# Retuning the planner of a fused mLSTM, token mixer and gated MLP kernel: later first transfers, filler products in shorter gaps, one score bank moved

## The chip, the cores and the metric

The kernel runs on one core of a Trainium2 chip. The metric is the device time of one execution in microseconds (us). Shown with the kernel are three executions of the version before, and one more that the hardware profiler recorded.

## The reference

Three stages follow each other. The first is an mLSTM attention over batch 2, 8 heads, 768 steps and head size 40; the reference runs it step by step with a running maximum `m` for the exponential gates:

```python
for t in range(S):
    m_new = np.maximum(f_gate[:, :, t] + m, i_gate[:, :, t])
    f_stab = np.exp(f_gate[:, :, t] + m - m_new)
    i_stab = np.exp(i_gate[:, :, t] - m_new)
    C = f_stab * C + i_stab * outer(vt, kt);  n = f_stab * n + i_stab * kt
    y[:, :, t] = sigmoid(o_gate) * (C @ qt) / max(abs(n . qt), 1)
```

Its output, heads side by side, is x (2 x 768 x 320). Then `u = x + (relu(x.T @ w_tok1) @ w_tok2).T` and `x = u + relu(u @ w_ch1) @ w_ch2`. Last comes a gated MLP: `h = gelu(x @ w_in)` is halved into u and v, v is normalised over its 512 columns and mixed over the sequence with `w_sg` (768 x 768), and `x + (u * v_s) @ w_out` is returned in float32.

## The kernel before, in words

The attention is done in chunks of 128 steps, 6 for each batch, 12 in all (n = 0 to 11). For each chunk `p1` forms the decay matrix (L685, one product for each half of the heads, then an exponential on ScalarE and a causal mask on GpSimd, L687), `p2` forms the scores k.q (L697, eight products, four for a half) and multiplies them into the decays (L698), and `p3` weighs the values (wv, L715), updates the state (L720 and on) and forms the output (L738, L740). Ahead of that, `gates` turns the gate inputs into cumulative sums and maxima: scans on VectorE, six products L587 that spread one row over the partitions, transposes L612, L618 and L633 on TensorE, a one-column product L623, and three products L647. `spread` (L595 to L606) writes the maxima, one head after the other, into MR, which L685 reads; its wide multiplications are L605.

The weights come as float64 words. `to_f32` makes float32 of them with one pass on ScalarE and four on VectorE (L501 to L507), and `split` cuts them into a high and a low part, so that three fast products do for one exact one; the low part is a wide subtraction on line L516 (L526 and L529 in `split_tails`, L536 for the float32 weights, L977 for v, L1009 for gs). Channel mixing (`ch_steps`, L833 to L850) and the gated MLP follow the attention; weights for later stages are loaded and converted beside it.

No instruction is issued where it is written. `Plan` records every operation with its engine, a cost and its dependences, and lays them out in time by a list scheduler (`order`), with due times from a first pass; `replay` runs the found order again under a little noise, and `best` tries a grid of parameters (how early transfers may be issued, a margin for TensorE, and `big`, the widest output in elements per partition that may go to GpSimd) and keeps the order with the smallest mean. Operations written with `flex` in place of `dve` may be put on GpSimd if their output has at most `big` elements. The plan takes TensorE to run at half rate until 6.6 us (`cold`, `slow`). To keep TensorE at work ahead of its first real product it issues fillers: 128x128 products of ones (L570) into bank 7 of PSUM, until something else writes that bank:

```python
t = max([free["PE"]] + [q.end + self.LAT for q in idle.pre])
while t + idle.dur * self.cold(t) < s + 0.05:
    done.append(self.filler(t))
    t += idle.dur * self.cold(t)
```

Transfers are all issued by SyncE, in the plan's order, at most eight in flight. In `load_chunk`, qk of a chunk is three transfers of 120 KB each (L672 twice, L674), kvo one of 504 KB (L678). Scores of chunk 0 go to PSUM banks 1 and 2, those of chunk 1 to banks 6 and 7, later ones to 1 and 2 in turn; p1 has bank 0 for all.

Of the kernel before, what the change touches and what calls it, by code (L numbers as in the profile page):

```python
# [42 lines left out]
def asf(t):  # L43
    return t.bitcast(F32)
# [33 lines left out]
class Plan:  # L78
# [158 lines left out]
    def order(self, ends=None, window=9.0, margin=0.0, big=999):  # L237
# [36 lines left out]
        for _ in ops:  # L274
# [22 lines left out]
            if e == "PE" and idle is not None:  # L297
                if any(r and r[0] == idle.outs[0][0] and r[3] < idle.outs[0][4] and idle.outs[0][3] < r[4] for r in o.outs):
                    idle = None
                else:  # L300
                    t = max([free["PE"]] + [q.end + self.LAT for q in idle.pre])
                    while t + idle.dur * self.cold(t) < s + 0.05:
                        done.append(self.filler(t))
                        t += idle.dur * self.cold(t)
            o.start = s
            free[e] = s + o.dur * (self.cold(s) if e == "PE" else 1.0)
# [3 lines left out]
            if o.name == "dma_start":  # L310
                queue = max(queue, free[e] + 0.75) + o.wire * (1.0 if queue < 65.0 else 0.8)
                o.end = queue + 0.55
                lanes.append(o.end)
                lanes.sort()
# [15 lines left out]
    def replay(self, done, rand):  # L330
# [9 lines left out]
        while True:  # L340
# [35 lines left out]
            if o.name == "dma_start":  # L376
                queue = max(queue, free[e] + 0.75) + o.wire * ((1.0 if queue < 65.0 else 0.8) + 0.1 * rand())
                end[o] = queue + 0.55 + 0.3 * rand()
                lanes.append(end[o])
                lanes.sort()  # L380
# [3 lines left out]

    def best(self, rounds=2, windows=(12.0, 16.0, 20.0, 25.0, 32.0), margins=(0.0, 0.3), bigs=(400, 999), trials=6):

# [35 lines left out]
def tile_mlstm_mixer_gmlp(  # L422
# [52 lines left out]
    def bank(banks):  # L475
        i = turn.get(banks, 0)
        turn[banks] = i + 1
        return ps[:, banks[i % len(banks)], :]
# [84 lines left out]
    def gates():  # L563
# [31 lines left out]
        def spread(b, m, mr, halves):  # L595
# [7 lines left out]
            for hf in range(halves):  # L603
                hs = slice(n * hf, n * hf + n)
                dve.tensor_tensor(out=mr[:, hs, :], in0=asf(st).unsqueeze(1).to_broadcast([128, n, 128]),  # L605
                                  in1=hm[b][:, hs].unsqueeze(2).to_broadcast([128, n, 128]), op=ALU.mult)  # L606
# [83 lines left out]
    def p2(n):  # L690
        E, qt, kt = E_s[n % 4], qT[n % NSET], kTm[n % NSET]
        for hf in range(2):
            p = bank((6, 7) if n == 1 else (1, 2)).rearrange("p (j t) -> p j t", j=4)
            for j in range(4):
# [473 lines left out]
```

## Time and profile before

| what | us |
|---|---|
| three executions | 366.25, 363.68, 366.04 (median 366.04) |
| the profiled execution | 365.41 |
| its span, first to last instruction | 363.6 |
| TensorE busy in the span | 357.3 (98%) |
| VectorE busy | 261.4 (72%) |
| ScalarE busy | 167.4 (46%) |
| GpSimd busy | 86.6 (24%) |

The profiled execution is 1.8 us longer than its span; that part lies outside the program's instructions. All times in the rows below count from the start of the span. A row of the timeline merges neighbours of one form: its start, the time from the first start to the last end, engine, line, operation, output<-inputs, a form (partitions x columns) and a count. A float32 product is recorded as two passes, so that the six fillers are x12. The bracket is the idle time of the engine ahead of the row and what ended it.

### The profile page before, as it was taken

Reading aid. Unit: us, or ns where it says so; the run is one execution under the profiler, and the core shown is the slowest. Engines: PE = TensorE matmul, PEld = TensorE weight load, DVE = VectorE, ACT = ScalarE, POOL = GpSimd, SP = SyncE. Lnnn points to the kernel's source line nnn. Section 1 sums busy time; section 2 is a strip of 40 time slices with the busy share of each in tenths; the row PEclk is TensorE's granted clock in tenths of the full one; section 3 lists DMA queues with packets and bytes.
Section 4 is the critical chain, followed back from the end, with each engine's and each line's share of the span. In section 5 each row is a group of like instructions: output and inputs, shape, how many; then the busy total and the mean of one; then the engine's idle time right before and its main releaser. Section 6 shows DMA issues by size and latency. Waiting matters only on the chain.

```text
span 363.6 us, 5959 instructions
## 1 busy us (share of the span) xinstructions
PE 357.3 (98%) x2257; PEld 343.6 (95%) x2257; DVE 261.4 (72%) x510; ACT 167.4 (46%) x377; POOL 86.6 (24%) x103
## 2 busy tenths in 40 slices
PE   7999999999999999999999999999999999999996
PEld 6998988998999999999999999999999999999995
DVE  4498888899888447794673359889898887454563
ACT  4488636767353235342352338754644444122230
POOL 3172325226120000120030006972124402010100
PEclk9999999999999999999999999999999999999999
DMA  5966447792580003000480000000000010010101
GB/s 159 289 257 214 145 133 275 227 321 62 176 342 0 2 0 115 2 0 3 146 303 0 3 0 2 0 0 2 1 2 0 2 54 1 2 54 3 54 0 56
DMA packets 11238, 30.96 MB, mean 85 GB/s; under 512 B 1481, under 2 KB 4233, under 8 KB 11209
## 3 DMA queue, kind: packets, MB, share of 16 engines
q1 hardware_dynamic: 11208, 30.57, 25.5%
q8 instruction: 18, 0.29, 0.3%
q14 instruction: 12, 0.09, 0.1%
HBM read 28.60 MB, written 1.97 MB: 84 GB/s over the span
## 4 chain that ended last, share of the span: by engine, by line
PE 95%; DVE 2%; DMA 1%; ACT 1%; SPq 0%; issue 0%
PE ps L697 6%; PE ps L850 6%; PE ps L848 6%; PE ps L849 6%; PE ps L740 5%; PE ps L835 5%; PE ps L834 5%; PE ps L833 5%; PE ps L1004 5%; PE ps L1003 5%; PE ps L1002 5%; PE ps L781 4%; PE ps L838 2%; PE ps L837 2%; PE ps L685 2%; PE ps L1020 2%
## 5 line engine op out<-in xcount | busy, mean ns | idle before, releaser
L784 ACT ACTIVATE a<-ps 128x384 fp32r<-128x384 f32 x48 | 23.6, 492 | 57.5 <-PE ps L838 57.0
L785 DVE SCALAR_TENSOR_TENSOR a<-ps,a 128x384 fp32r<-128x384 f32 x48 | 26.6, 554 | 27.1 <-ACT a L784 26.4
L788 DVE TENSOR_TENSOR nat<-ps,nat 128x320 f32<-128x320 f32 x48 | 22.3, 489 | 14.5 <-PE ps L850 7.3
L1002 PE MATMUL ps<-wsg,v 128*128 128x384 f32 x96 | 32.3, 337 | 0.0
L1003 PE MATMUL ps<-wsg,v 128*128 128x384 f32 x96 | 32.3, 337 | 0.0
L1004 PE MATMUL ps<-wsg,v 128*128 128x384 f32 x96 | 32.3, 337 | 0.0
L697 PEld LDWEIGHTS ps<-qk 120*128 120x128 f32 (+1 forms) x192 | 27.9, 209 | 2.5 <-DMA qk<-in_qk_dram 1.2
L697 PE MATMUL ps<-qk 120*128 120x128 f32 (+1 forms) x192 | 29.4, 296 | 0.7 <-DMA qk<-in_qk_dram 0.7
L687 POOL TENSOR_SCALAR_AFFINE_SELECT E<-E 128x512 f32<-128x512 f32 x24 | 17.0, 717 | 43.3 <-ACT E L686 37.0
L1008 ACT CAST gs<-g 128x384 fp32r<-128x384 f32 x16 | 8.2, 512 | 36.2 <-DVE g L1007 36.2
L740 PE MATMUL ps<-kvo,E 128*128 128x41 f32 x192 | 23.2, 279 | 0.0
L740 PEld LDWEIGHTS ps<-kvo,E 128*128 128x128 f32 x192 | 22.8, 192 | 0.1
L951 ACT ACTIVATE sq<-sq 128x384 f32<-128x384 f32 (+1 forms) x28 | 15.9, 570 | 10.3 <-DVE sq L950 10.0
L949 ACT ACTIVATE sq<-ps 128x384 f32<-128x384 f32 (+1 forms) x28 | 15.0, 536 | 12.2 <-PE ps L967 9.2
L1006 DVE SCALAR_TENSOR_TENSOR g<-ps,gln,bsg 128x384 f32<-128x384 f32 x16 | 9.8, 615 | 14.6 <-PE ps L1004 14.6
L950 DVE SCALAR_TENSOR_TENSOR sq<-sq,ps 128x384 f32<-128x384 f32 (+1 forms) x28 | 17.0, 606 | 3.5 <-ACT sq L949 3.2
L698 DVE TENSOR_TENSOR E<-ps,E 128x512 f32<-128x512 f32 x24 | 16.2, 682 | 3.0 <-PE ps L697 2.4
L1002 PEld LDWEIGHTS ps<-wsg,v 128*128 128x128 f32 x96 | 18.1, 188 | 0.0
L1004 PEld LDWEIGHTS ps<-wsg,v 128*128 128x128 f32 x96 | 18.0, 188 | 0.0
L1003 PEld LDWEIGHTS ps<-wsg,v 128*128 128x128 f32 x96 | 18.0, 188 | 0.0
L801 DVE TENSOR_TENSOR uT<-ps,uT 128x384 fp32r<-128x384 f32 x24 | 13.3, 553 | 6.5 <-ACT uT L800 6.5
L686 ACT ACTIVATE E<-ps 128x512 f32<-128x512 f32 x24 | 14.3, 596 | 6.0 <-PE ps L685 5.8
(346 smaller groups left out, 1128.0 us busy)
## 6 DMA issues: line engine op xcount, KB each, us to landing
kvo<-in_kvo_dram SPq DMA_DIRECT2D x12, 504.0 KB
qk<-in_qk_dram SPq DMA_DIRECT2D x36, 120.0 KB
rwin<-in_win_dram SPq DMA_DIRECT2D x5, 512.0 KB
rwsg<-in_wsg_dram SPq DMA_DIRECT2D x6, 384.0 KB
out_dram<-nat SPq DMA_DIRECT2D x12, 160.0 KB
rwo<-in_wout_dram SPq DMA_DIRECT2D x4, 320.0 KB
rw__129<-in_tok_dram SPq DMA_DIRECT2D x1, 768.0 KB
rw__131<-in_tok_dram SPq DMA_DIRECT2D x1, 768.0 KB
```

The lines of the kernel that those rows point to most:

```text
L697: mm(p[:, j, :], kt[jj][0:r, g, :], qt[0:r, g, :], start=True, stop=True)
L740: mm(psO[:, h, :], E[:, h // 4, h % 4, :], v1[:, h, :], start=(c == 0 and h == 0), stop=(h == H - 1))
L784: act.activation(out=hi, in_=p, func=AF.Relu)
L785: dve.scalar_tensor_tensor(out=lo, in0=p, scalar=0.0, in1=asf(hi), op0=ALU.max, op1=ALU.subtract)
L788: dve.tensor_tensor(out=nat[:, b, s], in0=p, in1=nat[:, b, s], op=ALU.add)
L833: mm(p, w[:, 0, ms], hi[:, k, ts], start=(k == 0), stop=False)
L848: mm(acc, a[:, 0, js], w[:, 0, :], start=(m == 0), stop=False)
L849: mm(acc, a[:, 0, js], w[:, 1, :], start=False, stop=False)
L850: mm(acc, a[:, 1, js], w[:, 0, :], start=False, stop=(m == 5))
L1002: mm(p, v[:, 0, ds_], wsg[s][:, 0, ts], start=(s == 0), stop=False)
L1003: mm(p, v[:, 0, ds_], wsg[s][:, 1, ts], start=False, stop=False)
L1004: mm(p, v[:, 1, ds_], wsg[s][:, 0, ts], start=False, stop=(s == NC - 1))
```

## The change

Four edits, all to what the planner is told. First transfers: one that starts while the queue stands between 3.5 and 12 us costs 1.3 times its wire time, and one that ends its wire time between 3.5 and 20 us lands 1.6 us later instead of 0.55, in `order` and in `replay`. Fillers: ahead of 7.0 us a filler is put in whenever 0.2 us are left, and it may push the next product back (`s = max(s, t)`); after that the rule is nearly the old one. The grid of `best` drops the window 12.0 and gains the margin 0.15. In `spread`, the wide multiplication is `flex`; in `p2`, only the first half of chunk 1 goes to bank 6 and the second half to banks 1 and 2 in turn, so that bank 7 is written by fillers until token mixing.

```diff
-                    while t + idle.dur * self.cold(t) < s + 0.05:
+                    while t + (0.2 if t < 7.0 else idle.dur * self.cold(t) - 0.05) < s:
                         done.append(self.filler(t))
                         t += idle.dur * self.cold(t)
+                    s = max(s, t)
...
-                queue = max(queue, free[e] + 0.75) + o.wire * (1.0 if queue < 65.0 else 0.8)
-                o.end = queue + 0.55
+                queue = max(queue, free[e] + 0.75)
+                queue += o.wire * (0.8 if queue > 65.0 else 1.3 if 3.5 < queue < 12.0 else 1.0)
+                o.end = queue + (1.6 if 3.5 < queue < 20.0 else 0.55)
...
-    def best(self, rounds=2, windows=(12.0, 16.0, 20.0, 25.0, 32.0), margins=(0.0, 0.3), bigs=(400, 999), trials=6):
+    def best(self, rounds=2, windows=(16.0, 20.0, 25.0, 32.0), margins=(0.0, 0.15, 0.3), bigs=(400, 999), trials=6):
...
-                dve.tensor_tensor(out=mr[:, hs, :], in0=asf(st).unsqueeze(1).to_broadcast([128, n, 128]),
+                flex.tensor_tensor(out=mr[:, hs, :], in0=asf(st).unsqueeze(1).to_broadcast([128, n, 128]),
...
-            p = bank((6, 7) if n == 1 else (1, 2)).rearrange("p (j t) -> p j t", j=4)
+            p = bank((6,) if n == 1 and not hf else (1, 2)).rearrange("p (j t) -> p j t", j=4)
```

The edits to `replay` are the same as the second piece, with its noise. The program has the same instructions as before but for one filler; their order and the engine of some change everywhere. Lines of the changed kernel from L386 on are three higher than those before (L570 is L573).

TensorE at the start of the program, before: gt, con and qk are the gate tiles, the constants and the q and k of a chunk (qk_75 chunk 0, qk_76 chunk 1); MR_72 and LR_69 go into the decays.

```order
L570 MATMUL ps_58<-gt_111 128x128 x6
L612 MATMUL ps_58<-con_59,gt_118 1x128
L587 MATMUL ps_58<-gt_115,con_59 128x128
L697 MATMUL ps_58<-qk_75 128x128
L618 MATMUL ps_58<-con_59,gt_120 1x128
L587 MATMUL ps_58<-gt_116,con_59 128x128
L697 MATMUL ps_58<-qk_75 128x128
L623 MATMUL ps_58<-gt_111,gt_121 128x1
L697 MATMUL ps_58<-qk_75 128x128 x2
L587 MATMUL ps_58<-gt_116,con_59 128x128
L685 MATMUL ps_58<-MR_72,LR_69 128x512
```

TensorE at the same place in the changed kernel:

```order
L573 MATMUL ps_58<-gt_111 128x128 x6
L615 MATMUL ps_58<-con_59,gt_118 1x128
L573 MATMUL ps_58<-gt_111 128x128
L590 MATMUL ps_58<-gt_115,con_59 128x128
L590 MATMUL ps_58<-gt_116,con_59 128x128
L621 MATMUL ps_58<-con_59,gt_120 1x128
L700 MATMUL ps_58<-qk_75 128x128 x2
L590 MATMUL ps_58<-gt_116,con_59 128x128
L688 MATMUL ps_58<-MR_72,LR_69 128x512
L626 MATMUL ps_58<-gt_111,gt_121 128x1
L700 MATMUL ps_58<-qk_75 128x128 x2
```

One filler now stands behind the first transpose, the second L587 (L590) moved ahead of the second transpose, and both ahead of the first score product; the first L685 (L688) comes before the one-column product.

SyncE's queue of transfers from the start, before:

```order
L541 DMA gin<-in_gates_dram 128x293
L542 DMA con<-in_gates_dram 128x268
L672 DMA qk<-in_qk_dram 40x768 x2
L674 DMA qk<-in_qk_dram 40x2x384
L678 DMA kvo<-in_kvo_dram 128x1008
L672 DMA qk<-in_qk_dram 40x768 x2
L674 DMA qk<-in_qk_dram 40x2x384
L496 DMA rw__129<-in_tok_dram 128x1536
L672 DMA qk<-in_qk_dram 40x768 x2
L674 DMA qk<-in_qk_dram 40x2x384
L678 DMA kvo<-in_kvo_dram 128x1008 x2
L496 DMA rw__131<-in_tok_dram 128x1536
```

And in the changed kernel:

```order
L544 DMA gin<-in_gates_dram 128x293
L545 DMA con<-in_gates_dram 128x268
L675 DMA qk<-in_qk_dram 40x768 x2
L677 DMA qk<-in_qk_dram 40x2x384
L675 DMA qk<-in_qk_dram 40x768 x2
L677 DMA qk<-in_qk_dram 40x2x384
L681 DMA kvo<-in_kvo_dram 128x1008
L675 DMA qk<-in_qk_dram 40x768 x2
L677 DMA qk<-in_qk_dram 40x2x384
L681 DMA kvo<-in_kvo_dram 128x1008
L499 DMA rw__129<-in_tok_dram 128x1536
L681 DMA kvo<-in_kvo_dram 128x1008
```

The values of chunk 0 (kvo) moved behind the qk of chunk 1, and the first token weights (rw) behind the kvo of chunk 1; the first five transfers stand as before.

GpSimd in the gated MLP's weights, before: wsg, win and v are the spatial weights, the input weights and the normalised half of h, each with its low part subtracted here.

```order
L974 TENSOR_TENSOR mv<-mv,mhalf 128x1
L516 TENSOR_TENSOR win<-wt,win 128x512
L536 TENSOR_TENSOR wsg<-rwsg,wsg 128x768
L516 TENSOR_TENSOR win<-wt,win 128x512
L977 TENSOR_TENSOR v<-v_178,v 128x512
L536 TENSOR_TENSOR wsg<-rwsg,wsg 128x768
```

In the changed kernel, VectorE at the weights of channel mixing; L788 is L785 of before (the low part of an activation) and L519 is L516:

```order
L788 SCALAR_TENSOR_TENSOR a<-ps,a 128x384
L507 SCALAR_TENSOR_TENSOR wt<-rc__207,wt 128x384
L519 TENSOR_TENSOR c__212<-wt,c__212 128x640
L507 SCALAR_TENSOR_TENSOR wt<-rc__209,wt 128x384
L788 SCALAR_TENSOR_TENSOR a<-ps,a 128x384
```

Of all outputs wider than 400 elements, none is left on GpSimd but the masks L687 and the memsets at the start: 23 wide subtractions (seven of L516, one of L526, two of L529, five of L536, eight of L977) moved to VectorE, among them that of c__212 and those of wsg, win and v shown. Six narrower operations moved the other way (two each of L715, L732 and L1009). The wide multiplications of `spread` (512 and 1024 elements) are on VectorE in both.

## Rows read from the trace of the kernel before

**Rows 1.** The page's first part: busy us (share of the span) xinstructions of each engine.
```profile
PE 357.3 (98%) x2257; PEld 343.6 (95%) x2257; DVE 261.4 (72%) x510; ACT 167.4 (46%) x377; POOL 86.6 (24%) x103
```

**Rows 2.** Who waited for whom, TensorE alone: us in total, times, longest.
```profile
PE ps L697 <- DMA qk<-in_qk_dram: 0.7, 2, 0.4
PE ps L685 <- ACT E L686: 0.6, 1, 0.6
PE ps L794 <- DVE nat L788: 0.3, 1, 0.3
```

**Rows 3.** The timeline of TensorE over the first 19 us.
```profile
1.10 2.93 PE L570 MATMUL ps<-gt 128*128 128x128 f32 x12 [1.10 <-DVE gt L569]
3.85 0.40 PE L612 MATMUL ps<-con,gt 128*1 128x128 f32 x1
4.37 0.79 PE L587 MATMUL ps<-gt,con 128*128 128x128 f32 x2
5.46 0.76 PE L697 MATMUL ps<-qk 80*128 80x128 f32 x2 [0.29 <-DMA qk<-in_qk_dram]
...
7.25 0.79 PE L697 MATMUL ps<-qk 120*128 120x128 f32 x2 [0.39 <-DMA qk<-in_qk_dram]
...
14.77 1.49 PE L697 MATMUL ps<-qk 120*128 120x128 f32 x6
16.05 0.63 PE L587 MATMUL ps<-gt,con 128*128 128x128 f32 x2
...
16.76 0.76 PE L685 MATMUL ps<-MR,LR 128*128 128x512 f32 x1
17.33 1.08 PE L697 MATMUL ps<-qk 120*128 120x128 f32 x8
18.24 0.38 PE L720 MATMUL ps<-wv,kvo 128*120 128x123 f32 x2
18.38 0.47 PE L685 MATMUL ps<-MR,LR 128*128 128x512 f32 x1
18.69 0.55 PE L720 MATMUL ps<-wv,kvo 128*120 128x123 f32 x4
```

**Rows 4.** Windows: length, busy (x) of PE, PEld, DVE, ACT, POOL, PEclk, DMA share, GB/s.
```profile
0.00:17.30 17.30, 15.39 (x62) 13.83 (x63) 8.59 (x27) 7.65 (x19) 4.28 (x11) 1.00 0.80 217
17.30:60.00 42.70, 42.67 (x334) 39.77 (x333) 36.89 (x67) 29.23 (x76) 19.72 (x27) 1.00 0.60 204
100.00:300.00 200.00, 200.00 (x1214) 194.50 (x1213) 147.95 (x280) 89.43 (x186) 45.20 (x48) 1.00 0.13 44
```

**Rows 5.** The timeline of the other engines over the first 19 us.
```profile
0.88 0.17 DVE L569 MEMSET gt<- 128x128 f32 x1 [0.88 <-PEq L1152]
1.12 0.38 DVE L558 MEMSET qk<- 120x384 f32 x1
10.15 0.47 ACT L705 ACTIVATE th<-kvo 128x320 f32<-128x320 f32 x1 [2.69 <-DMA kvo<-in_kvo_dram]
18.82 0.75 POOL L715 TENSOR_TENSOR wv<-kvo,wT 128x328 f32<-128x328 f32 x1
```

**Rows 6.** Groups by line and form: xcount | busy us, mean ns | idle before us <-releasers.
```profile
L977 POOL TENSOR_TENSOR v<-v,v 128x512 fp32r<-128x512 f32 x8 | 10.6, 1325 | 10.3 <-ACT v L976 10.3
L977 DVE TENSOR_TENSOR v<-v,v 128x512 fp32r<-128x512 f32 x4 | 2.7, 686 | 0.0
L536 DVE TENSOR_TENSOR wsg<-rwsg,wsg 128x768 fp32r<-128x768 f32 x1 | 0.9, 946 | 0.0
L516 DVE TENSOR_TENSOR c__206<-wt,c__206 128x384 fp32r<-128x384 f32 x1 | 0.6, 553 | 0.0
```

**Rows 7.** The timeline of three engines around one wide subtraction on GpSimd.
```profile
83.44 0.55 DVE L507 SCALAR_TENSOR_TENSOR wt<-rc__136,wt 128x384 int32<-128x384 int32 x1
83.44 2.22 POOL L529 TENSOR_TENSOR c__142<-wt,c__142 64x768 fp32r<-64x768 f32 x1 [0.28 <-ACT c__142 L527]
83.91 2.17 DVE L507 SCALAR_TENSOR_TENSOR wt<-rc__138,wt 128x384 int32<-128x384 int32 x1
87.30 0.41 PE L794 MATMUL ps<-con,nat 128*128 128x128 f32 x2 [0.32 <-DVE nat L788]
```

More of the change, by code (lines that the diff above doesn't have):

```diff
@@ L376, in replay @@
             if o.name == "dma_start":
-                queue = max(queue, free[e] + 0.75) + o.wire * ((1.0 if queue < 65.0 else 0.8) + 0.1 * rand())
-                end[o] = queue + 0.55 + 0.3 * rand()
+                queue = max(queue, free[e] + 0.75)
+                queue += o.wire * ((0.8 if queue > 65.0 else 1.3 if 3.5 < queue < 12.0 else 1.0) + 0.1 * rand())
+                end[o] = queue + (1.6 if 3.5 < queue < 20.0 else 0.55) + 0.3 * rand()
                 lanes.append(end[o])
```

## The prediction, made before the changed kernel was run

> **What bounds the kernel now.** I read the page's busy shares first [rows 1]: TensorE (PE) is busy for 357.3 of 363.6 us. The waits of PE come next [rows 2], and they are small: 0.7 us for q and k, 0.6 and 0.3 us later on. So hardly any time is idle, and what can be won must lie inside the busy time. The timeline of the first 19 us [rows 3] shows it. Passes of one form, 128 columns, run from 14.77 to 16.05 in six steps, 0.213 us each; eight of them from 17.33 to 18.24, 0.114 us each. From 17.33 us on PE works at twice its former rate: before that it had the lower of its two clock levels (1.2 GHz), after it the higher (2.4 GHz). The granted clock in the windows says 1.00 for both stretches [rows 4]; the spacing contradicts it for the first, and I go by the spacing. So PE spends the time from 1.10 to 17.33, 16.2 us, at the lower level, and each microsecond by which the clock rises sooner is worth half a microsecond, as long as PE has work at hand.
>
> What PE did before the rise: fillers from 1.10 and the first transpose, then an idle 0.12 us (3.85 + 0.40 to 4.37), 0.29 us ahead of 5.46 and 0.39 us ahead of 7.25; after that no row up to 17.33 has an idle mark [rows 3]. The three short pauses are what the change's filler rule and its later transfers aim at.
>
> **The change, part by part.** The sum is made against the profiled execution, 365.4 us (span 363.6 and 1.8 outside it). That lies 0.6 us under the median of the runs shown, 366.04; I add this at the end.
>
> *Start, fillers, first transposes.* In the changed order VectorE clears qk (0.38 us) before it makes the ones for the fillers [rows 5], so the fillers begin at about 1.48, not 1.10. Six of them and the way to the transpose took 2.75 us (1.10 to 3.85): the transpose comes at 4.23. The seventh filler is two passes, 0.43 us, and with the transpose's pass 0.21: L587 at 4.87 instead of 4.37. The second L587 and the second transpose follow (0.64), then the first score product, which needs only the first two parts of qk (there before 5.46), at 5.95 to 6.4. All this is without a pause, so PE runs unbroken from 1.48 to 6.4: 4.9 us, against 3.15 (1.10 to 4.25) before. Then the next score product needs the third part of qk, which ended a wait at 7.25 before; the five transfers up to it stand as they did, so I let it land then too, and PE has one pause of 0.8 us. At 7.25 both kernels have the same real products behind them (two L587, both transposes, one score product). The filler and the later start therefore cost nothing: they lie in time that ends with that transfer. Without this cover they would cost 0.5 us.
>
> *From 7.25 to the first L720.* By the two orders PE does the same products here, except that before, a third L685 (0.57 us, 16.76 to 17.33 [rows 3]) came ahead of L720, and now behind. Before: 18.24 - 7.25 = 11.0 us, so 10.4 now at the same clock. That is no gain by itself: the L685 is done a little later.
>
> *The clock.* The trace can't show when it will rise. One bound is no gain: the rise at 17.3 as now, or even later (each microsecond costs 0.5). The other is a rise in the first unbroken run, before 7.25: then all the work up to L720 runs at the higher level, and (17.3 - 7.25)/2 = 5.0 us are won. Longer unbroken work before 6.4, and a moment that no longer follows three pauses, speak for sooner; the second pause of 0.8 us, longer than any before, speaks against the first bound. I take the middle of 6.4 and 17.3, 11.9: (17.3 - 11.9)/2 = **-2.7 us**.
>
> The Trainium skill (TensorE: Matmul & The Clock Gate, Part 1) says that the throttled clock is the default, that activity releases it and that the moment differs from run to run; and it advises against this kind of work: the ramp's penalty is under 1% of a typical span, which one is not to fit to. By that the whole penalty here would be under 3.6 us and my step about -1.2 us. The trace has 16.2 us at the lower level [rows 3], half of that 8.1 us or 2.2%, so it disagrees, and I keep -2.7. With the run-to-run part the runs do fit: 366.25 to 363.68 is 2.6 us, what a rise 5 us sooner would give.
>
> *Do the transfers and VectorE let PE have that?* kvo of chunk 0 landed at 10.15 [rows 5]. It now stands behind the three qk transfers of chunk 1, 360 KB more; at the 217 GB/s of these 17 us [rows 4] that is 1.7 us: 11.8. With wv on GpSimd (0.75 us [rows 5]) L720 can start at 12.6; with the clock up at 11.9 PE gets there at 7.25 + 4.65 + (10.4 - 4.65)/2 = 14.8, so this is hidden by 2.2 us. Bounds of the landing: 10.15, and 13.5 if it took as long again. VectorE is busy 45.5 us of the first 60 [rows 4]; in 57.3 us that is 79%, still below PE. The first token weights now stand behind kvo of chunk 1 and two transfers more, 864 KB or some 4 us at the same rate; their first user L781 stands among the L740 of chunk 2 in the changed order, two chunks behind, so I count nothing; uncovered it would be at most those 4 us. The remaining swaps of SyncE's queue lie under stages in which PE waits for no transfer [rows 2]: no cost, and none can be gained.
>
> *Subtractions to VectorE.* 23 wide ones move. On VectorE they cost 0.69 (L977, eight: 5.5 us), 0.95 (L536, five: 4.7) and between 0.55 and 0.95, say 0.8, for the ten others (8.0) [rows 6]; six operations of about 0.55 go the other way (-3.3). VectorE gets 14.9 us more, 276 of 363. Most lie between 100 and 300 us, where it is busy 148 of 200 [rows 4]. Upper bound: all of it on the path, +14.9. Lower bound: one row says a little gain. While GpSimd made L529 (83.44 to 85.66), an L507 on VectorE took 2.17 us, where its twin just ahead took 0.55 [rows 7]; the 0.3 us that PE waited for VectorE at 87.30 came behind it and may go: -0.3. VectorE already carries 14 such subtractions with no other wait of PE for it in the waits [rows 2], so I stay near the low end: one of the moved ones, say 0.8 us, lands ahead of an L785 that a product waits for (in the changed order that of c__212 stands two rows ahead of one): **+0.8 us**.
>
> *No cost, no gain:* `spread` may go to GpSimd but doesn't (its outputs are wider than the limit chosen). Bank 7 kept free lets more fillers in, and none was put in there; the second half of chunk 1's scores now shares banks 1 and 2 with chunk 0, and waits for the multiplication L698 of that. That L698 belongs to the scores at the head of the queue, so it is done while PE makes the scores between; only where PE is fast from the start can a wait show, and I leave that to the first rival.
>
> Sum: 365.4 - 2.7 + 0.8 = 363.5; with the 0.6 by which the median lies above the profiled execution, **364.1 us**, 0.5% under 366.04. About 1% is what a measurement of this kernel tells from no change.
>
> **Rivals.**
> *Early rise.* The clock rises in the unbroken first run, by 6.4. For it: 4.9 us without a pause where there were 3.15. Then PE wins 5.0, but meets L720 at 7.25 + 5.2 = 12.45 just as kvo allows it (12.6), and the transfers that reuse the qk of chunk 0 have less room; I leave 4.4 of the 5.0: 365.4 - 4.4 + 0.8 + 0.6 = 362.4.
> *No sooner rise.* The pause of 0.8 us ahead of 7.25 undoes the fillers' work, and the rise comes at 17.3 or later. For it: before, PE also went ten microseconds without an idle mark from 7.25 and stayed at the lower level all that time [rows 3]. Then only the moved subtractions count: 365.4 + 0.8 + 0.6 = 366.8; a rise 1 us later still, 367.3.
> *VectorE becomes the bound: slower.* The place is the weight conversion beside channel mixing and the gated MLP, 100 to 300 us, where the products wait for L785 behind a subtraction. It decides once more than 2.7 us of the 14.9 come onto the path. With half of it: 365.4 - 2.7 + 7.5 + 0.6 = 370.8. Against it: 52 us of VectorE's 200 are free there [rows 4], and GpSimd no longer holds it up.
>
> **How the numbers follow.** Forecast 0.48, early rise 0.18, no sooner rise 0.24, VectorE the bound 0.10. The forecast's own range is 363 to 365.5 (rise between 9 and 14 us). The whole range goes from 362.0 (early rise with the waits' lower bound) to 367.3 (late rise), and leaves out half of VectorE's case and a third of the early rise and some of the tails. Faster by over 1% is under 362.4: half of the early rise and the edge of the forecast, 0.14. Slower by over 1%, above 369.7: most of VectorE's case, 0.07. Within 1%: 0.79.
>
> **What would show it.** Right: passes of 128 columns at 0.11 us by some 12 us in TensorE's timeline, one pause ahead of the third part of qk and none before it; first L720 near 15; VectorE busy some 272 to 277 us and PE's waits for it about 1 us. The clock step is wrong if the spacing is still 0.213 at 16 us (then no gain), or 0.11 at 7.5. The transfer step is wrong if L720 waits for wv or kvo; the step on VectorE if L848 to L850 or L833 wait for L785 by more than 2 us in sum.

## The result: 360.48 us, and the profile after

Median 360.48 us (four executions, 360.14 to 361.08) against 365.64 for the kernel before beside it (363.68 to 366.25): ratio 0.987, 95% interval [0.983, 0.991]. That is under the forecast's range (362.0 to 367.3). The profiled execution took 360.39, its span is 358.7: 4.93 less than before. Medians and ratios here and below leave out slow executions, those over 1.5% above the fastest of the same kernel. Lines from L386 on are three higher now.

The page's busy shares [rows 1], then who TensorE waited for [rows 2]: us in total, times, longest.

```profile
PE 350.9 (98%) x2259; PEld 338.9 (94%) x2259; DVE 266.6 (74%) x527; ACT 168.1 (47%) x377; POOL 57.0 (16%) x86
```
```profile
PE ps L700 <- DMA qk<-in_qk_dram: 0.9, 1, 0.9
PE ps L700 <- DVE E L701: 0.6, 1, 0.6
PE ps L836 <- DVE a L788: 0.5, 1, 0.5
PE ps L797 <- DVE nat L791: 0.3, 1, 0.3
PE ps L818 <- DVE hl L788: 0.3, 1, 0.3
```

TensorE has 6.4 us less busy time for the same products and one filler more. Its waits are longer than before, and still the kernel is faster. The start of TensorE's timeline [rows 3]:

```profile
1.51 2.93 PE L573 MATMUL ps<-gt 128*128 128x128 f32 x12 [1.51 <-DVE gt L623]
4.23 0.42 PE L615 MATMUL ps<-con,gt 128*1 128x128 f32 x1
4.44 0.64 PE L573 MATMUL ps<-gt 128*128 128x128 f32 x2
4.87 0.72 PE L590 MATMUL ps<-gt,con 128*128 128x128 f32 x4
5.43 0.27 PE L621 MATMUL ps<-con,gt 128*1 128x128 f32 x1
5.54 0.39 PE L700 MATMUL ps<-qk 80*128 80x128 f32 x2
6.82 0.49 PE L700 MATMUL ps<-qk 120*128 120x128 f32 x2 [0.89 <-DMA qk<-in_qk_dram]
...
10.79 2.25 PE L700 MATMUL ps<-qk 80*128 80x128 f32 x18
12.88 0.59 PE L723 MATMUL ps<-wv,kvo 128*120 128x123 f32 x4
...
14.16 1.02 PE L743 MATMUL ps<-kvo,E 128*128 128x41 f32 x8
```

Four passes of L590 take 4.87 to 5.43, and L621's single pass only 0.11 (5.43 to 5.54): the spacing changes from 0.21 to 0.11 inside the row of L590, at 5.1 us. From there TensorE works at the higher level (eighteen passes from 10.79 in 2.09 us), which before it reached at 17.33. The first pause comes later, 0.89 us ahead of 6.82, and the clock stays up through it. The first window [rows 4] and GpSimd's step ahead of L723 (kvo was there at 10.63, forecast 11.8 [rows 5]):

```profile
0.00:17.30 17.30, 14.72 (x105) 13.71 (x105) 13.10 (x34) 10.76 (x29) 6.08 (x14) 1.00 0.75 243
```
```profile
10.63 0.74 POOL L718 TENSOR_TENSOR wv<-kvo,wT 128x328 f32<-128x328 f32 x1 [1.47 <-DMA kvo<-in_kvo_dram]
```

TensorE makes 105 passes in the first 17.3 us, not 62. Where the time went, by the starts of the same passes in both timelines:

| pass | before | after | difference |
|---|---|---|---|
| first L720 | 18.24 | 12.88 | -5.36 |
| 65th of the scores L697 | 35.6 | 31.2 | -4.44 |
| 129th | 61.2 | 56.6 | -4.63 |
| 161st | 78.1 | 72.4 | -5.77 |
| first L963 | 211.2 | 206.4 | -4.90 |
| end | 363.6 | 358.7 | -4.93 |

The prize falls in the first 13 us. Some is lost to the wait of 0.56 us at 23.58 (L700 for L701); some comes in where before's wait of 0.60 for E [rows 2] is not there; 0.27 and 0.52 are lost again to L788 at 98.1 and 102.8.

The rise at 17.33 is that of one execution of before. Of the 95 others that stand beside the runs below, 43 show a granted clock, averaged over the span, of 0.984 to 0.995, where the profiled one shows 0.998. Since the column reads 1.00 ahead of the first rise, the clock of these 43 had risen and fallen again. They took no less time (median 365.23 against 365.06 for the rest).

### The profile page after: what moved, and what is told of

It reads as the page before. It is cut to its first block, busy times and chain, and to the rows that moved or that the text cites. A ratio compares the mean times of both kernels' runs of the same rounds, so it can differ in the third digit from the quotient of the medians.

```text
span 358.7 us, 5943 instructions
## 1 busy us (share of the span) xinstructions
PE 350.9 (98%) x2259; PEld 338.9 (94%) x2259; DVE 266.6 (74%) x527; ACT 168.1 (47%) x377; POOL 57.0 (16%) x86
## 4 chain that ended last, share of the span: by engine, by line
PE 90%; DVE 4%; DMA 3%; issue 1%; ACT 1%; SPq 0%
PE ps L853 6%; PE ps L852 6%; PE ps L851 6%; PE ps L700 5%; PE ps L743 5%; PE ps L1007 5%; PE ps L836 5%; PE ps L1006 5%; PE ps L1005 5%; PE ps L837 5%; PE ps L838 5%; PE ps L784 3%; PE ps L840 2%; PE ps L841 2%; PE ps L1023 2%; PE ps L1021 2%
## 5 line engine op out<-in xcount | busy, mean ns | idle before, releaser
L787 ACT ACTIVATE a<-ps 128x384 fp32r<-128x384 f32 x48 | 23.6, 491 | 51.8 <-PE ps L841 51.4
L788 DVE SCALAR_TENSOR_TENSOR a<-ps,a 128x384 fp32r<-128x384 f32 x48 | 26.4, 554 | 22.0 <-ACT a L787 21.7
L791 DVE TENSOR_TENSOR nat<-ps,nat 128x320 f32<-128x320 f32 x48 | 22.3, 490 | 15.2 <-PE ps L853 7.3
L700 PE MATMUL ps<-qk 120*128 120x128 f32 (+1 forms) x192 | 27.0, 277 | 1.5 <-DMA qk<-in_qk_dram 0.9
L700 PEld LDWEIGHTS ps<-qk 120*128 120x128 f32 (+1 forms) x192 | 25.2, 191 | 2.8 <-DMA qk<-in_qk_dram 1.1
L952 ACT ACTIVATE sq<-ps 128x384 f32<-128x384 f32 (+1 forms) x28 | 14.9, 534 | 19.5 <-PE ps L970 14.2
L976 POOL TENSOR_SCALAR mv<-mv 128x1 f32<-128x1 f32 x12 | 4.5, 373 | 98.2 <-DVE mv L975 98.2
L1009 DVE SCALAR_TENSOR_TENSOR g<-ps,gln,bsg 128x384 f32<-128x384 f32 x16 | 9.9, 616 | 13.1 <-PE ps L1007 13.0
L701 DVE TENSOR_TENSOR E<-ps,E 128x512 f32<-128x512 f32 x24 | 16.2, 685 | 3.5 <-PE ps L700 2.4
```

Of the source, the lines that this page charges most:

```text
L700: mm(p[:, j, :], kt[jj][0:r, g, :], qt[0:r, g, :], start=True, stop=True)
L787: act.activation(out=hi, in_=p, func=AF.Relu)
L788: dve.scalar_tensor_tensor(out=lo, in0=p, scalar=0.0, in1=asf(hi), op0=ALU.max, op1=ALU.subtract)
L791: dve.tensor_tensor(out=nat[:, b, s], in0=p, in1=nat[:, b, s], op=ALU.add)
```

## The experiments

The kernels named b_ and a_ are before and after with the planned order kept, edited ahead of the loop in `issue` (`seq` is the planned list, `o.i` an operation's number in the program); p_ kernels change the planner and are planned anew. Inserted lines shift line numbers by a few; the text names the lines by those of the parent kernel.

### Is it the unbroken start?

```diff
+pe = [o for o in seq if o.eng == "PE"]
+at = next(o for o in pe if o.name == "transpose")
+seq.insert(seq.index(at) + 1, self.filler(0.0))              # b_one_filler
...
+for i, n in ((k, 1), (k + 1, 2), (k + 4, 1)):                # b_four_fillers, k: first transpose
+    for _ in range(n):
+        seq.insert(seq.index(pe[i]) + 1, self.filler(0.0))
...
+f = [o for o in seq if o.a is self.idle.a]
+seq.remove(f[6])                                             # a_no_seventh
+for o in f[3:]: seq.remove(o)                                # a_three_fillers
```

> The kernel before, its order kept, with one filler more behind the first transpose; it closes the first of the three short pauses (0.12 us), so that TensorE has no pause from 1.10 us to about 5.2; the two later ones (0.29 and 0.39 us) stay. Theory (the short pauses kept the clock at the lower level): the passes of 128 columns come at 0.11 us before 5.5 us, the first L720 starts at 12.5 to 14 instead of 18.24, and the time falls by 3.5 to 5 us, to some 361 us. Rival (the earlier rise came from something else in the new order, such as the later start of the fillers or the real products that stand among them): the spacing stays 0.21 beyond 10 us and the time is within 1 us of 365.6.

> The kernel before, its order kept, with four fillers that close all three pauses ahead of 7.3 us (one behind the first transpose, two behind the first L587, one behind the next L587). Theory (short pauses kept the clock low): rise by 5.5 us as with one filler, and the same time within 0.6 us, as one unbroken stretch up to 5 us is enough. Rival (what counts is the whole stretch up to 7.3 us): this kernel rises early and the one with a single filler doesn't; 361 against 365.6 us.

> The changed kernel without its seventh filler, the one behind the first transpose; the inputs of the next products are there by then, so no pause should arise. Theory (only the pauses count): rise by 5.5 us and 360.5 us within 0.6. Rival (the number of fillers, or the seventh one itself, made the rise): spacing 0.21 beyond 10 us, 364 to 366 us.

> The changed kernel with only its first three fillers: TensorE stops at about 2.8 us and waits 1 us or more for the first transpose; from there its products stand as in the changed kernel. Theory (unbroken work from the start raises the clock early): the rise comes after 10 us, the first L723 at 16 us or later, the time is 363.5 to 366. Rival (the fillers have no part in it, the reordered real products do it): rise by 7 us and 360.5 us within 0.8.

| kernel | higher level from | first L720 / L723 | ratio to before |
|---|---|---|---|
| b_one_filler | 5.9, lost at 8.9, again 15.6 | 17.19 | 1.000 [0.998, 1.002] |
| b_four_fillers | 7.2 | 15.48 | 1.003 [0.999, 1.006] |
| a_no_seventh | 6.7, lost from 23.6 to 27.0 | 12.59 | 0.989 [0.986, 0.992], 360.97 us |
| a_three_fillers | 13.1 | 15.50 | 0.993 [0.990, 0.996], 362.49 us |

In the changed order the fillers matter: with three (1.22 us of pause ahead of the first transpose) the rise came 8 us later, at a cost of 2.0 us, less than the 3 or more that were expected. The seventh doesn't: the time stayed as expected, though the rise came at 6.7 and not by 5.5. Each rise is read from one profiled execution. In the order of before an early rise is worth nothing, which neither theory had. TensorE of b_one_filler, then three windows of it (the third number from the end is the granted clock):

```profile
5.83 0.46 PE L701 MATMUL ps<-qk 80*128 80x128 f32 x2 [0.73 <-DMA qk<-in_qk_dram]
6.13 0.27 PE L622 MATMUL ps<-con,gt 128*1 128x128 f32 x1
...
7.39 0.49 PE L701 MATMUL ps<-qk 120*128 120x128 f32 x2 [0.77 <-DMA qk<-in_qk_dram]
...
14.27 1.49 PE L701 MATMUL ps<-qk 120*128 120x128 f32 x6
```
```profile
6.00:8.80 2.80, 2.04 (x15) 1.68 (x15) 1.49 (x5) 0.56 (x2) 0.00 (x0) 1.00 0.74 183
9.35:15.50 6.15, 6.00 (x27) 5.61 (x26) 3.67 (x9) 3.60 (x10) 1.28 (x2) 0.50 1.04 267
15.70:20.00 4.30, 4.30 (x37) 4.17 (x36) 2.34 (x4) 3.09 (x9) 1.95 (x3) 1.00 0.82 271
```

A faster TensorE meets the same transfers sooner, waits longer for them (0.73 and 0.77, where before waited 0.29 and 0.39), and then the clock falls back: granted 0.50 from 9.35 to 15.5. In b_four_fillers it stays up, and another thing stops TensorE. Its ScalarE, and TensorE's row:

```profile
7.32 0.40 ACT L592 ACTIVATE gt<-gt,gin 128x128 f32<-128x128 f32 x1
10.36 0.47 ACT L711 ACTIVATE th<-kvo 128x320 f32<-128x320 f32 x1 [2.64 <-DMA kvo<-in_kvo_dram]
10.74 0.39 ACT L592 ACTIVATE gt<-gt,gin 128x128 f32<-128x128 f32 x1
```
```profile
11.17 0.49 PE L593 MATMUL ps<-gt,con 128*128 128x128 f32 x2 [1.65 <-ACT gt L592]
```

L711 here is L705 of before: it waits for kvo at the head of ScalarE's queue from 7.72 to 10.36, and the gates' step L586 (L592 here) stands behind it and runs as soon as it is done. The same pair stands in before (L705 at 10.15 [rows 5]); there TensorE was slow enough not to notice.

### What stands behind the early clock

```diff
+for early, urgent in ((117, 65), (143, 89)):                 # b_four_late, b_late_only
+    i, j = seq.index(at[early]), seq.index(at[urgent]) + 1   # L705 and the first L500
+    late = [at[early]]
+    for o in seq[i + 1:j]:
+        if any(p in late for p in o.pre):
+            late.append(o)
+    seq[i:j] = [o for o in seq[i:j] if o not in late] + late
...
+seq.remove(sp[15])                                           # b_rw_late also: sp is SyncE's queue,
+seq.insert(seq.index(sp[18]) + 1, sp[15])                    # and (202, 239) in the list above
...
+seq.remove(at[117])                                          # a_early_th
+seq.insert(seq.index(at[70]), at[117])                       # L708 ahead of an L589
```

> The kernel before with the four fillers of b_four_fillers, and two steps of ScalarE that wait for a transfer put later in its queue: L705 of chunk 0 (waits for kvo, stood ahead of two L586) behind L648, and the first L500 (waits for the first token weights, stood ahead of two L686) behind the second of these. Theory now (two locks: the clock must rise early, and nothing that waits for a transfer may stand ahead of what TensorE needs next): the waits of 1.65 and 0.89 us of b_four_fillers go, the first L720 comes at 12.8 to 14 us, the time is 361 to 362.5 and no run is beyond 364. Rival (other waits take their place, or the clock falls back anyway): 364 to 366 as b_four_fillers.

> The kernel before with only the two moves in ScalarE's queue, without fillers. Theory (two locks): no gain by itself, since TensorE at the lower clock reaches the third L587 just when L586 is done; within 0.8 us of 365.1, the spacing 0.21 beyond 12 us. Rival (ScalarE's queue alone was the cost): 361 to 363.

> The changed kernel with L708 of chunk 0 (L705 of before) put back ahead of an L589 in ScalarE's queue, as the kernel before has it; all else stands. Theory (two locks): kvo lands at 10.6 us, so the L589 that was done at 9.6 comes at 11.1, TensorE waits 1 to 1.8 us for it behind 9.8 us, and the time rises to 361.5 to 363. Rival (the place of this step doesn't matter): 360.5 within 0.4, no new wait of TensorE over 0.3 us before 13 us.

> b_four_late with one more move: the second transfer of token weights (768 KB) stands behind the qk of chunk 3 in SyncE's queue, no longer ahead of it, and its conversions follow it on ScalarE and VectorE. In b_four_late TensorE waited 2.03 us for that qk at 23.79, and the clock then fell to the lower level from 24.93 to 31.58. Theory (the early clock is kept only where no wait of about 2 us follows; the order made for late transfers sees to that): the wait at 23.8 shrinks below 0.7 us, the clock stays up, the profiled span falls by 3 to 5 us to 360 to 362, the median to 361.5 to 363.5. Rival (the queue of transfers as a whole is too slow for the fast start in this order): the wait moves to another transfer, the clock falls again, 364 to 367.

b_four_late: 1.002 [0.999, 1.005], a miss. Both waits are gone, the first L720 came at 14.17, 4.1 us sooner; then this, TensorE's timeline and the windows around it:

```profile
23.79 0.68 PE L712 MATMUL ps<-qk 120*128 120x128 f32 x4 [2.03 <-DMA qk<-in_qk_dram]
...
25.14 3.55 PE L755 MATMUL ps<-kvo,E 128*128 128x41 f32 x16
```
```profile
8.00:16.00 8.00, 7.65 (x63) 7.27 (x62) 6.63 (x16) 5.37 (x13) 2.23 (x3) 1.00 0.99 263
25.00:31.00 6.00, 6.00 (x23) 5.31 (x23) 0.86 (x3) 1.65 (x6) 1.47 (x3) 0.50 0.84 239
32.00:40.00 8.00, 8.00 (x65) 7.36 (x64) 7.36 (x15) 5.81 (x14) 1.39 (x3) 1.00 0.35 112
```

TensorE reached the scores of chunk 3 sooner than their qk, waited 2.03 us, and then the clock stood at 0.50 from 24.8 to 31.5 us: sixteen passes of L740 (L755 here) took 3.55 us, where eight take 1.02 in after's timeline above. All was lost again (span 365.2). The Trainium skill (TensorE: Matmul & The Clock Gate, "HAM oscillation — how this bites in real kernels") tells of this pattern, a stretch of products that ends in a wait for a transfer, and the next stretch slow behind it. This trace agrees, though its wait of 2.03 us is shorter than those that the Trainium skill tells of there.

b_rw_late moves that qk ahead of a token weight: the wait was 1.03 (expected: below 0.7), the clock stayed up in the profiled execution, span 362.3, median 363.80, ratio 0.995 [0.992, 0.997]. The theory holds in direction; span and median are each 0.3 above their bounds, with 2.1 us of waits for qk and 1.06 for the mask of E left. b_late_only, without fillers, has 0.9995 [0.996, 1.003]: no gain, as expected. Its profiled execution (370.5 us) lies far above its median, so its time says nothing, but its trace shows the clock. TensorE, and a window of it:

```profile
5.49 0.28 PE L627 MATMUL ps<-con,gt 128*1 128x128 f32 x1
5.61 0.38 PE L596 MATMUL ps<-gt,con 128*128 128x128 f32 x2
7.49 0.49 PE L706 MATMUL ps<-qk 120*128 120x128 f32 x2 [1.50 <-DMA qk<-in_qk_dram]
```
```profile
8.00:11.60 3.60, 3.60 (x17) 3.49 (x18) 1.79 (x7) 1.00 (x2) 0.61 (x1) 0.53 0.85 242
```

The expectation (0.21 beyond 12 us) misses. With the products and the six fillers of before, and a pause of 0.16 us ahead of 5.20, the passes come at 0.11 us from 5.3; the clock then falls behind the wait of 1.50, and once more behind one of 1.83. So the order of before can rise early without more fillers, and when it rises isn't fixed by that order.

a_early_th puts L705's old place into the changed kernel: 0.997 [0.993, 1.000], median 363.73, profiled span 361.5. Its TensorE and windows:

```profile
11.38 0.49 PE L594 MATMUL ps<-gt,con 128*128 128x128 f32 x2 [1.86 <-ACT gt L593]
```
```profile
7.70:9.20 1.50, 1.50 (x13) 1.46 (x14) 1.39 (x6) 0.31 (x1) 0.65 (x1) 1.00 1.04 273
12.90:15.30 2.40, 2.40 (x12) 2.40 (x13) 2.37 (x5) 0.92 (x4) 0.50 (x1) 0.50 1.01 415
```

The wait is 1.86 us, about what was expected; that the clock then falls as well was not, and the median lies 0.7 above the expected bound. One step of ScalarE in its old place takes most of the gain back.

### The subtractions on VectorE, and the waits left

```diff
+for o in seq:                                                # a_subs_pool: the 23, and two L519 of 384
+    if o.i in back and o.a is not self.idle.a: o.eng = "POOL"
...
+for early, urgent in ((146, 163), (554, 653), (641, 861), (714, 881)):   # a_late_conv: moved as above
...
+seq.remove(sp[15])                                           # a_late_rw
+seq.insert(seq.index(sp[18]) + 1, sp[15])
+con.eng = "ACT"                                              # a_late_rw_con: con is SyncE's second transfer
+seq.remove(con); seq.insert(0, con)
+at[644].eng = "DVE"                                          # a_late_all: behind at[881]
```

> The changed kernel with the wide subtractions that the change moved to VectorE put back on GpSimd, each at its place in the order. If they cost 0.8 us on VectorE, as predicted: the waits of TensorE for L788 (0.5 and 0.3 us at 98 and 103 us) go, and the time falls by 0.4 to 0.8 us, to 359.7 to 360.1. Rival (GpSimd's longer hold of the port they share costs as much as it gives): unchanged within 0.3 us, or slower by up to 1 us, with waits of TensorE for VectorE elsewhere.

> The changed kernel with four weight conversions (L507 at 21.5, 71.5 and 96.6 us, L510 at 101.0) each put behind the operation of VectorE that TensorE waits for (L701, L791, L788). Theory (TensorE's waits for VectorE come from such conversions ahead of urgent steps): the waits at 73.8, 98.1 and 102.8 us (0.34, 0.27, 0.52) go, and 0.6 to 1.1 us of the time; at 23.6 us the transfer of qk lands at 24.2 anyway, so that wait (0.56) changes its name more than its size. Rival (other waits take their place): within 0.3 us of 360.5.

> a_late_conv and the second transfer of token weights behind the qk of chunk 3. Theory: qk of chunk 3 lands some 3 us sooner (768 KB at 250 GB/s), the wait at 23.6 us goes as well: 0.3 to 0.6 us under a_late_conv, some 359.2. Rival (the values of chunk 3 or the token weights, now later, end a wait instead): as a_late_conv or slower.

> a_late_rw, and the transfer of the constants is issued by ScalarE at the start instead of SyncE, so that all qk transfers are issued 0.4 us sooner. If the third part of qk of chunk 0 (waits of 0.9 us at 6.8 in the changed kernel) is held by the issuing: 0.3 to 0.5 us under a_late_rw, some 358.8. Rival (the transfer itself is slow, or ScalarE's start is delayed and the gates with it): no gain, or 0.4 us slower.

> a_late_rw_con, and the low part of c__146 (L519) moved from GpSimd to VectorE behind the two L788 that TensorE waits for at 101 us (0.4 us, while GpSimd's subtraction stretched them to 1.25 us). If GpSimd's hold on the port made that wait: 0.2 to 0.4 us under a_late_rw_con, some 358.9. Rival: unchanged within 0.2 us.

| kernel | median | span | ratio to before |
|---|---|---|---|
| a_subs_pool | 360.20 | 358.1 | 0.987 [0.983, 0.990] |
| a_late_conv | 359.69 | 358.2 | 0.984 [0.982, 0.987] |
| a_late_rw | 359.59 | 358.1 | 0.986 [0.983, 0.989] |
| a_late_rw_con | 359.22 | 357.9 | 0.984 [0.982, 0.986] |
| a_late_all | 360.00 | 358.5 | 0.986 [0.984, 0.988] |

a_subs_pool: the two waits for L788 went and the span of the profiled execution fell by 0.54 us. The median fell by 0.28, within the rival's 0.3, and the ratio is the same as the changed kernel's: that the moved subtractions cost half a microsecond on the path is read from the waits, and the times don't show it. VectorE of the changed kernel ahead of the wait at 102.76:

```profile
99.98 0.95 DVE L532 TENSOR_TENSOR c__142<-wt,c__142 64x768 fp32r<-64x768 f32 x1
100.97 1.26 DVE L510 SCALAR_TENSOR_TENSOR wt<-rc__147,wt 128x384 int32<-128x384 int32 x1
102.16 1.01 DVE L788 SCALAR_TENSOR_TENSOR a<-ps,a 128x384 fp32r<-128x384 f32 x2
```

A subtraction and a conversion, neither urgent, stand ahead of L788. a_late_conv puts the conversions behind: all four waits, at 23.6, 73.8, 98.1 and 102.8, are gone, a new one of 0.45 for L788 stands at 107.2 behind two other conversions, and the median falls by 0.8. I had expected the wait at 23.6 to become one for qk; it did not, so a_late_rw had nothing to win there. a_late_rw_con has the lowest median, but its interval overlaps with a_late_conv's, and whether the constants' transfer helps stays open. The clock rose at about 7.8 us in the profiles of these two and at 4.8 in that of a_late_rw, and at the end that made no difference: after the earlier rise TensorE meets the qk of chunk 0 sooner and waits 0.8 us. a_late_all misses, and its expectation had the wrong place: TensorE's wait left in a_late_rw_con (0.41) is at 107.0, not at 101. The two L788 at 100.65 still take 1.25 us with no subtraction on GpSimd beside them, so GpSimd's was not what stretched them; the subtraction, now on VectorE ahead of the L788 at 107, made the last wait longer (0.63). a_late_rw_con beats the kernel before. Its median is 1.3 us under the changed one's, but the two were not run side by side and their ratios' intervals overlap, so that it beats that one too isn't shown.

### One edit undone, planned anew

```diff
-while t + (0.2 if t < 7.0 else idle.dur * self.cold(t) - 0.05) < s:      # p_old_fill
+while t + idle.dur * self.cold(t) < s + 0.05:
-    s = max(s, t)
...
-queue += o.wire * (0.8 if queue > 65.0 else 1.3 if 3.5 < queue < 12.0 else 1.0)
+queue += o.wire * (1.0 if queue < 65.0 else 0.8)                        # p_old_wire, in replay too
-o.end = queue + (1.6 if 3.5 < queue < 20.0 else 0.55)
+o.end = queue + 0.55
...
-flex.tensor_tensor(out=mr[:, hs, :], in0=asf(st).unsqueeze(1).to_broadcast([128, n, 128]),
+dve.tensor_tensor(out=mr[:, hs, :], in0=asf(st).unsqueeze(1).to_broadcast([128, n, 128]),
-p = bank((6,) if n == 1 and not hf else (1, 2)).rearrange("p (j t) -> p j t", j=4)   # p_old_bank, with the line above
+p = bank((6, 7) if n == 1 else (1, 2)).rearrange("p (j t) -> p j t", j=4)
...
+    if o.a is not self.idle.a and o.flex and o.eng == "POOL" and elems(o.k["out"]) > 400:
+        o.eng = "DVE"                                                    # p_bank_dve: p_old_bank and this
```

> The changed kernel with the filler rule of before, planned anew: one of the four edits undone. The plan now has six fillers and none behind the first transpose, and the other three edits. Theory (early clock by the fillers, kept by an order made for late transfers): short pauses return ahead of 7 us, the rise comes late in most executions, and the order alone gives part of the gain as in a_three_fillers: 361.5 to 364, with a wider spread than the 1 us of the changed kernel. Rival (the fillers have no part in it): 360 to 361.2.

> The changed kernel with the transfer times of before in the plan, planned anew. The fillers stand as in the changed kernel, but products, ScalarE's steps and transfers are ordered for data that lands sooner than it does. Theory (two locks): the clock rises early, then TensorE runs into waits for qk, kvo or the gates of 1 to 3 us in all before 26 us, and may lose the clock again: 361.5 to 364.5. Rival (what the plan thinks of transfers doesn't matter once the fillers are in): 360 to 361.2, waits below 33 us as in the changed kernel (1.7 us).

> The changed kernel with the score banks and the engine of the spreads of before, planned anew. As predicted these two edits cost and give nothing by themselves: 360 to 361.5, with an early rise. Rival (the free bank is what lets the fillers do their work): the rise comes after 10 us, or waits for the bank appear, 362 to 365.

> p_old_bank with its order kept and the 22 wide subtractions that it has on GpSimd put on VectorE, each at its place. In p_old_bank L748 on VectorE took 2.08 us beside L529 on GpSimd (83.8 us), and TensorE waited 1.46 us for the step behind it at 86.5, and 1.03 and 0.93 us at 101.2 and 76.7. Theory (GpSimd's hold on the port they share made these waits): they shrink to under 0.4 us each, and the time falls by 2 to 3.5 us, to 362.5 to 364. Rival (VectorE is simply late there, and 15 us more work make it later): 366 or more.

p_old_fill: 0.986 [0.982, 0.990], median 359.94, with six fillers and the higher level from 6.0 us. That is below both expectations: the new filler rule isn't needed, as this order has no long pause at the start anyway. p_old_wire: 0.999 [0.996, 1.003], no gain. Its profiled execution (366.66) is 2.3 above its median. It too rises early (by 7 us) and is 3.8 us ahead of before at 61 us; it loses most of that in one place. Its ScalarE and VectorE there, TensorE's rows, and the window behind them:

```profile
73.03 0.90 ACT L503 ACTIVATE wt<-rc__140 128x768 f32<-128x768 f32 x1 [2.99 <-DMA rc__140<-in_ch_dram]
74.67 0.15 ACT L744 ACTIVATE dn<-ps 128x8 f32<-128x8 f32 x1
```
```profile
73.96 0.56 DVE L504 TENSOR_SCALAR wt<-wt 128x768 f32<-128x768 f32 x1 [3.38 <-ACT wt L503]
76.27 0.48 DVE L791 TENSOR_TENSOR nat<-ps,nat 128x320 f32<-128x320 f32 x1
```
```profile
76.90 0.41 PE L797 MATMUL ps<-con,nat 128*128 128x128 f32 x2 [2.37 <-ACT th L708]
...
78.32 0.72 PE L688 MATMUL ps<-MR,LR 128*128 128x512 f32 x1 [0.79 <-ACT E L689]
```
```profile
78.60:81.50 2.90, 2.90 (x14) 2.74 (x14) 1.86 (x4) 1.51 (x3) 1.58 (x2) 0.50 0.98 396
```

The bracket of L797 names L708, but what L797 transposes is nat, which L791 finished at 76.75. Behind it again is a ScalarE step that waits for a transfer, L503 (a conversion of channel weights): L744 stands behind it on ScalarE, its follower L504 stands ahead of the steps to nat on VectorE, and the clock falls behind TensorE's wait. Five of p_old_wire's seven executions show a granted clock of 0.999 or 1.000, and their median, 364.20, is only 0.7 under before's 364.90, so the fall isn't the whole of it.

p_old_bank: 1.003 [1.001, 1.005], 366.12 us, also without gain, which I had at no cost. It rises early (at 4.9) and is 2.6 us ahead of before at 61 us. Its plan keeps 22 wide subtractions on GpSimd, and TensorE waits 3.5 us for L791 and 0.93 for ScalarE behind 76 us. VectorE and GpSimd ahead of the longest of these waits (1.46 at 86.48):

```profile
83.84 2.08 DVE L748 TENSOR_TENSOR nat<-tn,dn 128x320 f32<-128x320 f32 x1
85.85 0.48 DVE L791 TENSOR_TENSOR nat<-ps,nat 128x320 f32<-128x320 f32 x1
```
```profile
83.78 1.80 POOL L529 TENSOR_TENSOR c__141<-wt,c__141 64x768 fp32r<-64x768 f32 x1 [4.89 <-issue]
```

L748 takes 2.08 us beside L529. In p_bank_dve, with the subtraction on VectorE, the same operation (L752 there):

```profile
81.96 0.49 DVE L752 TENSOR_TENSOR nat<-tn,dn 128x320 f32<-128x320 f32 x1
82.48 0.95 DVE L533 TENSOR_TENSOR c__141<-wt,c__141 64x768 fp32r<-64x768 f32 x1
```

The span of the profiled execution falls by 3.1 us to 362.4 (2.1 of it behind 61 us), the median by 1.8 to 364.28, 0.3 above the expected bound; ratio 1.000 [0.997, 1.003], which overlaps with p_old_bank's. So GpSimd's hold is shown for this step, but the expected 2 to 3.5 us only for the span: 0.98 us of wait is left, as the subtraction now stands ahead of L791 itself. The Trainium skill (SBUF — State Buffer, "SBUF: two separate sides") says that VectorE, in an operation with two inputs in SBUF, and GpSimd, in one that reads SBUF, share a port pair, which the one that starts first keeps for the whole instruction while the other blocks. L529 starts first (83.78), and 2.08 against 0.49 agrees.

The fourth edit, the grid of `best`, is in all p_ kernels and was not undone alone; what it gives stays open.

## Why the prediction was wrong

*The step that failed is the clock's:* "I take the middle of 6.4 and 17.3, 11.9: (17.3 - 11.9)/2 = **-2.7 us**". The rise came at 5.1, inside the first unbroken run, and the passes around 7.5 come at 0.11 us, the sign that I had named for a wrong clock step. The first L720 came 5.36 us sooner, not the 3.4 that the forecast's 14.8 means; without the L685 that now comes later (0.57) that is 4.8 for the clock. The bound of -5.0 was right in size. So the mechanism was right, and its term was mis-sized by some 2.1; I set between two bounds what the trace could not show, and gave the early bound 0.18. The other 1.5 us by which 360.48 lies under 364.1 are, as far as known, the 0.6 added for the median, the wait for E and part of the +0.8.

*The early rise's rival* names the mechanism. Its time, 362.4, was 1.9 too high; most of that is 0.6 held back for waits, the wait for E that went (0.60), and 0.6 added for before's median, where after's lies only 0.1 above the profiled execution.

*The reason for the rise* was half right. Fillers that stop 1.2 us too soon delay it by 8 us (a_three_fillers). That the three short pauses held it isn't shown: p_old_fill rises at 6.0 without the new rule, and b_late_only at 5.3 with the fillers and products of before. In the order of before an early rise is worth nothing: it does not last (b_one_filler, b_late_only and, by their granted clock, 43 of 95 executions of before itself), or a wait behind ScalarE's queue takes the gain (b_four_fillers).

*"The remaining swaps of SyncE's queue ... no cost, and none can be gained"*, and bank and spread at nothing: this failed too. With the transfer times undone and the rest kept, or bank and spread together, nothing is won (p_old_wire, p_old_bank). The edits don't add up: each makes the planner deal the order anew, so these runs don't tell which of the changed places counts. That the order counts is shown for one step of ScalarE (a_early_th); that the package got an order in which no step waiting for a transfer stands long ahead of what TensorE needs next is read from its waits (0.89 us at most) and not tested further. I read [rows 5] for when kvo lands, and not for who stands behind L705.

*Subtractions:* +0.8 has the size of the waits of 0.27 and 0.52 for L788 that appeared, but a_late_conv removes these without moving a subtraction, and putting them back gives 0.28 to 0.54. VectorE's sum was wrong: 14.9 us more were forecast, 5.2 measured (266.6, not 272 to 277), because other operations on VectorE became shorter. Five conversions of win, before and after:

```profile
L504 DVE SCALAR_TENSOR_TENSOR wt<-rwin,wt 128x512 int32<-128x512 int32 x5 | 6.9, 1395 | 0.0
L507 DVE SCALAR_TENSOR_TENSOR wt<-rwin,wt 128x512 int32<-128x512 int32 x5 | 3.3, 683 | 0.0
```

With the order kept and only the engine of the subtractions changed, the same form takes 1.24 us in p_old_bank and 0.68 in p_bank_dve, and 22 subtractions more leave VectorE's busy time nearly as it was (265.6, then 266.1). I counted the end of GpSimd's hold for one row only, at -0.3. In p_old_bank's order it was worth up to 2.1 us of the span; in the changed kernel's own order the return of the subtractions to GpSimd costs no time (a_subs_pool). PE's waits for VectorE were 1.7 us, not about 1.

*Transfers of kvo, the cover of fillers, the one pause ahead of the third part of qk:* as forecast or a little better (kvo at 10.63, not 11.8, and no wait of L720 for it; one pause, 0.89 us, that ends at 6.82). The first token weights stand behind three more transfers of qk, not two; the 864 KB count all three.

## What to carry to other kernels

A clock that rises sooner is a change of speed for one engine: ask for each queue beside it what it waits for, and which step the fast engine needs stands behind that, for the profile of the slow kernel hides all these waits. When a planner makes the order, price the order that comes out (the first waits on each engine), not the edits, and put conversions behind the operations that TensorE waits for. Where the trace can't place a threshold, work out the time at both bounds and let the chances, not the middle, carry it.

## What was not expected of the hardware

The clock, once up, came down again behind short waits, and the window's granted clock shows it (0.50), while the same column says 1.00 for the slow stretch ahead of the first rise. Seen: 1.86 us of wait, then low from 12.3 to 15.7 (a_early_th); 2.03, low from 24.8 to 31.5 (b_four_late); 2.37 and soon 0.79, low from 78.5 to 81.8 (p_old_wire); 0.73 and 0.77 with 1.1 us of work between, low from 8.9 to 15.6 (b_one_filler); 1.50 and later 1.83, low from 8.3 to 11.6 and from 25.3 to 35.5 (b_late_only); and 0.57, low from 23.6 to 27.0 (a_no_seventh). Not followed by a fall: 0.56 and 0.89 (after), 1.31 and 1.46 (p_old_bank), 1.65 (b_four_fillers). So the length of one wait doesn't tell whether the clock falls. What sets how long it stays low, or when it first rises (4.8 to about 7.8 us in the profiled executions of after's order with six or seven fillers, 17.3 and 5.3 in before and b_late_only, whose products come in the same order), stays open. After's executions spread over 0.9 us, before's over 2.6 beside it; of after's four, three show a granted clock of 1.000 and the slowest 0.995. A clock that neither comes late nor falls would explain the narrow spread, and wasn't tried by itself.
